# Side work of an output phase, rescheduled: one turn and two differences or splits a step, two more token tiles loaded into operands' places, their norm in place

## The chip, the cores and the metric

The kernel runs on one core of one Trainium2 chip. Its time is device time in microseconds of one execution. The profile was taken of one further execution of the same program. Engines are named as in the profile: PE (TensorE matmul), PEld (its weight loads), DVE (VectorE), ACT (ScalarE), POOL (GpSimd) and SP (SyncE, which here only issues DMAs).

## The reference

One adaLN-conditioned block over 2048 tokens of width 640, all float32: a state-space convolution (S4), then a gated feed-forward layer of width 1728.

```python
h = _layernorm(x) * (1 + ca) + sa
x = x + ga * _A_ref(h, ...)            # long convolution by FFT, plus u * Dskip
h = _layernorm(x) * (1 + cb) + sb
# _B_ref
gate = jnp.einsum("bsd,df->bsf", h, w1)
up = jnp.einsum("bsd,df->bsf", h, w3)
out = jnp.einsum("bsf,fd->bsd", _silu(gate) * up, w2)
x = x + gb * out
```

The change touches the seam between the two layers: z, the convolution's last transform, is brought back, added to x, normalized and turned for the feed-forward matmuls.

## The kernel before

The convolution runs first and leaves its spectrum `zs` in DRAM. The feed-forward layer then works in two **pairs** of token chunks. A chunk is 512 tokens, four **token tiles** of 128. The width 640 is five k-tiles of 128, the width 1728 fourteen f-tiles, the last of them half full. For precision each float32 operand is split into two float32r parts, a high one (a cast on ACT) and a low one (a subtraction on DVE), and each product takes three matmuls of 128 x 512.

In a pair the gate and up products of most f-tiles are made by a seven-product scheme (`seven`) that needs, beside the chunks' operands A and B, their differences T1, T2, T4 (`x_sums`, then `x_sum_split`). The results h stay in SBUF. Then comes the **output phase** of the pair (`outputs`, L1217): 28 steps, one for each of 14 f-tiles for the first chunk (c = 0) and then for the second (c = 1). The matmuls of a step take h and w2 of one f-tile into five accumulators, 15 matmuls (10 in a step of the last f-tile, which comes as the twelfth of each chunk, steps 11 and 25).

In the output phase of the first pair, PE, DVE, ACT, POOL and SP's stream keep the order in which the code is written (`InOrder`). Each step n writes, in this order:

- `load(n + 4)`: the DMA of w2 for four steps later, issued by ACT (two half DMAs for the last f-tile);
- `operands(n + 1)`: the next step's casts gh (w2) and uh (h) on ACT, and the low parts gl and ul on DVE. Each has two buffers;
- one of the first chunk's leftover adds (`late.pop`), steps 15 to 19;
- `side(n)`: the side work below;
- the matmuls of step n, which stand on PE behind the side work's.

The side work prepares the second pair (`prepare`, L1305) by tables of step numbers. Token tiles 0 to 3 become chunk A, 4 to 7 chunk B:

- `x_get` (L970, `gets`): SP loads z of a token tile from `zs`, and for tiles 4 to 7 x as well (those of 0 to 3 are loaded earlier). z needs 640 KB. A tile with `homes` takes two operands' places of 64 x 2 x 128 a DMA, ten DMAs of 64 KB. A tile without takes a buffer A of pool `tz`, five DMAs of 128 KB; the four buffers A also hold h of the first ten f-tiles, three to a buffer, so one comes free every three steps.
- `x_mid` (L984, `mids`): 16 small matmuls into two PSUM banks of `psG`, which has three; DVE adds them to x (xm), takes the statistics (st, mv), POOL makes the factors (rs) and stores x to `xs` with a DMA of its own.
- `x_norm` (L999, `norms`): one ACT instruction makes the normalized tile. Its four places are T41, T21, T11 and T31.
- `turn_a`, `turn_b` (`x_turn`, L1014): for one k-tile, four transposes on PE into one `psG` bank, then on ACT the modulation (into `room`) and the high part, on DVE the low part.
- `x_sums` (L1039), `x_sum_split` (L1048): four subtractions on DVE for each of two indices i; then for each difference a cast on ACT and a subtraction on DVE.

Every DMA of SP and ACT takes one of eight semaphores (DMAHW0 to DMAHW7) in turn, and waits until the DMA that had this semaphore before has landed. SP and ACT share the eight. This is called a **lane** below. A DMA that waits holds up all that stands behind it on its engine.

At the last step of chunk c = 0 (step 13) x of the four tiles is loaded back from `xs` into places (`xr`), and one accumulator is copied by ACT to `ob`, which the leftover work turns into place for the output's last 128 columns. The phase runs from 593.07 us, the first matmul of step 0, to 709.68 us, where the second pair's first product begins.

The lines quoted in the profile as L108 are a recorder's call, through which all of this phase goes; groups are told apart by tiles. The name T stands for all of T1 to T4.

Of the kernel before, what the change touches and what calls it, by code (L numbers as in the profile page):

```python
# [9 lines left out]
F32 = mybir.dt.float32  # L10
# [3 lines left out]
OP = mybir.AluOpType  # L14
# [3 lines left out]
P = 128  # L18
# [11 lines left out]
KD = D // P  # L30
# [83 lines left out]
def tile_kernel(ctx: ExitStack, tc: tile.TileContext, a):  # L114
    nc = tc.nc
    V, S, G, PE = nc.vector, nc.scalar, nc.gpsimd, nc.tensor
# [564 lines left out]
    def x_tile():  # L681
        return xp.tile([P, D], F32, name="xm", bufs=6)
# [112 lines left out]
    xp = None  # L795
# [122 lines left out]
    def room(i):  # L918

        return wq.tile([P, 512], F32, name=f"s{i}")  # L920
# [49 lines left out]
    def x_get(j, x, loaded=False, homes=None):  # L970

        if homes:
            zs_ = [pair_tile(n, F32).rearrange("p a b -> p (a b)")[:, :768].rearrange("p (b d) -> p b d", b=2)
                   for n in homes]
        else:
            zs_ = [z_tile()]
        with tc.issue_after(zlast[0].ins):
            if not loaded:
                SQ.dma_start(x, a["x"][j * P:(j + 1) * P, :])
            for i, z in enumerate(zs_):  # L980
                z_load(z, j, range(NDC), SQ, 2 * i)
        return [x, [zs_[b * len(zs_) // 4][:, b % (4 // len(zs_))] for b in range(4)]]
# [13 lines left out]
        got.extend(ln_stats(xp, x))  # L996
        G.dma_start(xs[j], x)

    def x_norm(j, got, tiles):  # L999

        x, _, rstd, bias = got
        xn = xn_tile(j % 4)
        S.activation(xn, x, AF.Identity, scale=rstd, bias=bias)
        tiles.append(xn)

# [27 lines left out]
    def turn_a(q, tiles, k, g):  # L1033
        xraw["A", k], xop["A", k] = x_turn(q, tiles, k, k if k < 4 else 8, g)

    def turn_b(q, tiles, k, g):
        xraw["B", k], xop["B", k] = x_turn(q, tiles, k, 4 + k if k < 4 else 8, g)

    def x_sums(i):  # L1039

        b11, b21, b12, b22 = xraw["A", i], xraw["A", i + 2], xraw["B", i], xraw["B", i + 2]
        V.tensor_tensor(b11, b12, b11, op=OP.subtract)
        V.tensor_tensor(b12, b22, b12, op=OP.subtract)
        V.tensor_tensor(b22, b22, b11, op=OP.subtract)
        V.tensor_tensor(b21, b21, b22, op=OP.subtract)
        xraw["T1", i], xraw["T2", i], xraw["T4", i] = b11, b22, b21

    def x_sum_split(i, names=("T1", "T2", "T4")):  # L1048
        for n in names:
            xop[n, i] = x_split(f"{n}{i}", xraw[n, i])  # L1050
# [27 lines left out]
    def fetch(f, name):  # L1078
        ahead[f, name] = weight(f, name)
# [137 lines left out]
    def outputs(q0, order, hs, side, last):  # L1217


        seq = [(c, f) for c in range(2) for f in order]  # L1220
        n_all, raws, ops, xr, accs, late = len(seq), {}, {}, [], [], []

        def load(n, q=None):
            if n < n_all:
                raws[n] = weight(seq[n][1], "w2", q)

        def gate(n):
            if n < n_all and last and seq[n][0]:
                G.tensor_tensor(raws[n][:, :512], raws[n][:, :512], gbr, op=OP.mult)

        def operands(n):
            if n < n_all:
                c, f = seq[n]
                ops[n] = out_operands(raws.pop(n), hs[c][f], f)

        def tail(q, ob, x):

            pt = bank(1)
            for i in range(4):
                PE.transpose(pt[:, i * P:(i + 1) * P], ob[:, i * P:(i + 1) * P], ident)  # L1240
            for i in range(4):
                V.tensor_tensor(x[i][:, 512:], pt[:, i * P:(i + 1) * P], x[i][:, 512:], op=OP.add)

        in_order[0] = True
        for n in range(4):
            load(n)
        gate(0)
        gate(1)
        operands(0)
        in_order[0] = False  # L1250
        yield
        in_order[0] = True
        for n, (c, f) in enumerate(seq):
            q, pos = q0 + c, n % NFT
            load(n + 4, S)
            operands(n + 1)
            gate(n + 2)
            if late and pos > 0:
                late.pop(0)()
            if pos == (13 if c == 0 else 10):  # L1260
                xr = [x_tile() if c else x_place(n) for n in ("T40", "T20", "T10", "T30")]
                for i in range(4):
                    SQ.dma_start(xr[i], xs[4 * q + i])
            if pos == 0:
                acc = {k: bank(0) for k in (4, 0, 1, 2, 3)}
            side(n)
            terms = ops.pop(n)
            for k in (4, 0, 1, 2, 3):
                for i, (hh, w) in enumerate(terms):
                    lhs, rhs = (hh[:, k * P:(k + 1) * P], w[:, :512]) if k < 4 else (w[:, 512:], hh)  # L1270
                    PE.matmul(acc[k], lhs, rhs, start=(pos == 0 and i == 0),
                              stop=(pos == NFT - 1 and i == len(terms) - 1))
                if pos < NFT - 1:
                    continue

                if k == 4:
                    ob = room(8) if c == 0 or last else xp.tile([P, 512], F32, name="idle", bufs=1)
                    S.activation(ob, acc[4], AF.Copy, scale=modT[:, 2, 4:5])
                    continue
                if last and c:  # L1280
                    V.tensor_tensor(xr[k][:, :512], acc[k], xr[k][:, :512], op=OP.add)
                else:
                    og = hs[c][order[10 + k]]
                    V.tensor_tensor(og, acc[k], gbr, op=OP.mult)
                    late.append(lambda x=xr[k], og=og: V.tensor_tensor(x[:, :512], og, x[:, :512], op=OP.add))
                if c == 0 or not last:
                    continue
                if k == 1:
                    tail(q, ob, xr)
                for i in ((), (0, 1), (2,), (3,))[k]:  # L1290
                    x_out(4 * q + i, xr[i])
            if pos == NFT - 1 and not (c and last):
                def rest_of(q=q, ob=ob, x=xr):
                    tail(q, ob, x)
                    for i in range(4):
                        x_out(4 * q + i, x[i])
                late.append(rest_of)
        side(n_all)
        in_order[0] = False
        yield  # L1300
        for t in late:
            t()
            yield

    def prepare(q0, g, x4):  # L1305


        steps, got, tiles = {}, {}, ([], [])

        def at(n, fn):  # L1310
            steps.setdefault(n, []).append(fn)

        mids = (3, 5, 6, 7, 9, 11, 14, 16)
        norms = (5, 7, 8, 9, 12, 13, 16, 18)
        gets = (0, 0, 1, 2, 3, 5, 7, 10)
        homes = (("xA0", "xA1"), ("xA2", "xA3"), ("xA4", "xB2"), ("xB3", "xB4"))
        for i, n in enumerate(norms):
            at(n, lambda i=i: x_norm(4 * q0 + i, got[i], tiles[i // 4]))
        for i, n in enumerate(gets):
            if i < 4:  # L1320
                at(n, lambda i=i: got.__setitem__(i, x_get(4 * q0 + i, x4[i], True, homes[i])))
            else:
                at(n, lambda i=i: got.__setitem__(i, x_get(4 * q0 + i, x_tile())))
        for k, n in enumerate((10, 10, 11, 11, 12)):
            steps.setdefault(n, []).insert(k % 2, lambda k=k: turn_a(q0, tiles[0], k, g))
        for k, n in zip((4, 0, 2, 3, 1), (20, 20, 21, 21, 22)):
            at(n, lambda k=k: turn_b(q0 + 1, tiles[1], k, g))
        for i, n in enumerate(mids):
            at(n, lambda i=i: x_mid(4 * q0 + i, got[i], g))
        at(24, lambda: fetch(NFT - 1, "wg"))  # L1330
        at(25, lambda: [fetch(0, n) for n in ("wg", "wu")])
        at(22, lambda: x_sums(0))
        at(23, lambda: x_sum_split(0, ("T1", "T2")))
        at(23, lambda: x_sums(1))
        at(24, lambda: x_sum_split(0, ("T4",)))
        at(24, lambda: x_sum_split(1, ("T1",)))
        at(25, lambda: x_sum_split(1, ("T2", "T4")))

        def side(n):
            for fn in steps.get(n, ()):  # L1340
                fn()
        return side
# [147 lines left out]
```

## Time and profile before

| what | us |
|---|---|
| three runs | 977.24, 978.68, 983.92 |
| their median | 978.68 |
| the profiled execution's own time | 978.73 |
| its span in the profile | 976.6 |
| output phase of the first pair in it | 593.07 to 709.68 |

Times inside the profile count from the start of its span. In a row of the timeline the first number is the start, the second the time from the first start to the last end of the instructions merged in the row, and brackets show how long the engine was idle before it and what ended that. A waits row gives the engine that waits, whom it waited for, the total in us, how often, and the longest. PE's own durations overlap (a matmul is shown as 0.39 us while the next starts 0.227 us later), so what a step costs is read from starts.

### The profile page before, as it was taken

Reading aid. Unit: us, or ns where it says so; the run is one execution under the profiler, and the core shown is the slowest. Engines: PE = TensorE matmul, PEld = TensorE weight load, DVE = VectorE, ACT = ScalarE, POOL = GpSimd, SP = SyncE. Lnnn points to the kernel's source line nnn. Section 1 sums busy time; section 2 is a strip of 40 time slices with the busy share of each in tenths; the row PEclk is TensorE's granted clock in tenths of the full one; section 3 lists DMA queues with packets and bytes.
Section 4 is the critical chain, followed back from the end, with each engine's and each line's share of the span. In section 5 each row is a group of like instructions: output and inputs, shape, how many; then the busy total and the mean of one; then the engine's idle time right before and its main releaser. Section 6 shows DMA issues by size and latency. Waiting matters only on the chain.

```text
span 976.6 us, 19962 instructions
## 1 busy us (share of the span) xinstructions
PE 899.5 (92%) x7924; PEld 675.1 (69%) x7924; DVE 704.7 (72%) x1225; ACT 534.6 (55%) x732; POOL 284.1 (29%) x300
## 2 busy tenths in 40 slices
PE   5886788999999997899999999999899999999997
PEld 2442456666666665577888887678688888888786
DVE  5687868999999985678566665675886666664674
ACT  4658578999999933356433332464543333323432
POOL 2832424445544301321222210321142222200341
PEclk9656757999999999999999999999999999999999
DMA  9571273766765788692211115966221121114342
GB/s 271 178 282 68 111 178 102 201 174 204 213 181 176 204 203 243 209 310 97 84 55 54 55 41 149 266 192 209 88 94 55 66 90 54 53 49 132 98 163 108
DMA packets 103888, 140.68 MB, mean 144 GB/s; under 512 B 20884, under 2 KB 62996, under 8 KB 103796
## 3 DMA queue, kind: packets, MB, share of 16 engines
q1 hardware_dynamic: 93012, 113.58, 38.9%
q10 hardware_dynamic: 8480, 18.09, 5.9%
q0 software_dynamic: 2304, 7.74, 2.3%
q8 instruction: 62, 1.02, 0.4%
q14 instruction: 30, 0.25, 0.1%
HBM read 107.92 MB, written 31.46 MB: 143 GB/s over the span
## 4 chain that ended last, share of the span: by engine, by line
PE 64%; ACT 12%; DVE 10%; DMA 7%; issue 3%; SPq 2%; POOL 1%; ACTq 0%; DVEq 0%; POOLq 0%
PE ps L108 46%; PE p L593 6%; ACT cs L142 3%; PE pz L635 3%; PE pt L562 3%; DMA A<-zs 3%; PE pa L455 2%; DMA s<-in_s_dram 2%; PE pk L544 2%; ACT A L142 2%; ACT L142 1%; ACT ph L142 1%; SPq L108 1%; DMA us<-u 1%; DVE E L520 1%
## 5 line engine op out<-in xcount | busy, mean ns | idle before, releaser
L108 DVE TENSOR_TENSOR s<-ps,s 128x512 f32<-128x512 f32 x138 | 94.9, 688 | 83.1 <-PE ps L108 82.9
L108 ACT CAST gh<-rw 128x640 fp32r<-128x640 f32 x87 | 63.4, 728 | 127.9 <-PE ps L108 85.4
L108 DVE TENSOR_TENSOR gl<-rw,gh 128x640 fp32r<-128x640 f32 x87 | 77.9, 895 | 69.5 <-ACT gh L108 69.3
L108 POOL TENSOR_TENSOR S<-rw 128x256 f32<-128x256 f32 x46 | 36.1, 786 | 225.2 <-DVE S0l L108 160.9
L593 PE MATMUL p<-uk,s 128*64 128x256 f32 x640 | 82.2, 401 | 16.0 <-DMA s<-in_s_dram 5.4
L108 PE MATMUL ps<-gh,uh 128*128 128x512 f32 x224 | 88.3, 394 | 0.0
L108 PE MATMUL ps<-gl,uh 128*128 128x512 f32 x224 | 88.2, 394 | 0.0
L108 PE MATMUL ps<-xA,gh 128*128 128x512 f32 x280 | 87.5, 391 | 0.4 <-ACT xA L108 0.4
L491 POOL TENSOR_TENSOR ph<-thi,iota 128x1376 int32<-128x1376 int32 x20 | 50.0, 2503 | 123.9 <-DVE A L531 90.6
L108 PE MATMUL ps<-gh,ul 128*128 128x512 f32 x208 | 81.1, 390 | 0.0
L593 PEld LDWEIGHTS p<-uk,s 128*64 128x64 f32 x640 | 46.6, 142 | 42.7 <-issue 8.1
L142 ACT ACTIVATE A<-pa 128x1024 f32<-128x1024 f32 (+1 forms) x80 | 64.5, 815 | 18.5 <-PE pa L455 18.3
L108 PEld LDWEIGHTS ps<-xA,gh 128*128 128x128 f32 x280 | 52.3, 188 | 12.9 <-issue 1.2
L527 DVE TENSOR_TENSOR A<-A,ph 128x1024 f32<-128x1024 f32 x40 | 54.5, 1363 | 0.9
L562 PE MATMUL pt<-s,K 128*64 128x128 f32 x640 | 51.0, 300 | 3.9 <-ACT uk L145 3.9
L108 PE MATMUL ps<-xA,gl 128*128 128x512 f32 x140 | 54.5, 389 | 0.0
L520 DVE TENSOR_TENSOR E<-A,cs 128x1024 f32<-128x1024 f32 x40 | 53.4, 1335 | 0.6 <-PE pk L544 0.6
L544 PE MATMUL pk<-E 128*32 128x64 f32 x1280 | 46.6, 239 | 4.0 <-DVE E L523 3.0
L108 PEld LDWEIGHTS ps<-gl,uh 128*128 128x128 f32 x224 | 42.6, 190 | 9.2
L635 PE MATMUL pz<-Y,i 64*128 64x128 f32 x640 | 47.3, 288 | 1.7 <-ACT zt L145 1.6
L108 PEld LDWEIGHTS ps<-gh,uh 128*128 128x128 f32 x224 | 42.5, 190 | 9.0
L635 PEld LDWEIGHTS pz<-Y,i 64*128 64x128 f32 x640 | 39.7, 190 | 12.6 <-issue 9.2
(242 smaller groups left out, 2231.9 us busy)
## 6 DMA issues: line engine op xcount, KB each, us to landing
rw<-in_w_dram ACTq DMA_DIRECT2D x44, 320.0 KB
us<-u SPq DMA_DIRECT2D x16, 640.0 KB
s<-in_s_dram SPq DMA_DIRECT2D x40, 256.0 KB
i<-in_i_dram SPq DMA_DIRECT2D x40, 256.0 KB
rw<-in_wg_dram SPq DMA_DIRECT2D x31, 320.0 KB
rw<-in_wu_dram SPq DMA_DIRECT2D x28, 320.0 KB
uk<-us SPq DMA_DIRECT2D x32, 256.0 KB
zs<-zt SPq DMA_DIRECT2D x32, 256.0 KB
```

Of the source, the lines that this page charges most:

```text
L108: ins = fn(*args, **kw)
L142: return tc.keep_in_program_order(S.activation(*args, **kw))
L455: keep(PE.matmul(ps[:, rr, :8 * n], lx[rows, s // SPC, s % SPC // 2, :], table[rows].rearrange("p j b -> p (j b)"), start=True, stop=True, ...
L491: hold(G.tensor_tensor(p[:, :, b0:], bc(thi[:, sl], 2, NPG - b0), bc(iota, 1, 2 * SD), op=OP.mult))
L520: keep(V.tensor_tensor(EC[s][:, :, 1:3, :], AA[s][:, :, 1:3, :], mid(cs[s]), op=OP.mult))
L527: keep(V.tensor_tensor(A[:, :, 1:3, :], A[:, :, 1:3, :], mid(ph[s]), op=OP.mult))
L544: keep(PE.matmul(pk[dq * 32:dq * 32 + 32, g, :], x[:, g * 4 + dq, 1, :], x[:, g * 4 + dq, 0:3:2, :], start=(st == 0), stop=(st == 1), tile ...
L562: keep(PE.matmul(pt[c * 64:c * 64 + 64, g, :], kk[:, g, :], s1[:, c, :], start=True, stop=True, tile_position=(0, c * 64)))
L593: keep(PE.matmul(p2[par * 64:par * 64 + 64, pi, c, :], s2[:, pi * 2 + par, c * 64:c * 64 + 64], uk[:, 0:kn + 1:kn, f, :], start=True, stop ...
L635: ins = keep(PE.matmul(pz[:, par, (g % 2) * 2 + pi, :], i1[r, pi, c, :], Y[r, pi, c, :], start=(c == 0), stop=(c == 1), tile_position=(par ...
```

## The change

All of it is in the first pair's output phase, but for `ob` of the last chunk, and no instruction is computed otherwise than before.

- **gets** go from steps 0, 0, 1, 2, 3, 5, 7, 10 to 0, 0, 1, 2, 3, 4, 4, 6. Tiles 4 and 5 get homes, T40 with T20 and T10 with T30, and so ten DMAs in the place of five.
- **mids** go from 3, 5, 6, 7, 9, 11, 14, 16 to 3, 4, 5, 6, 8, 9, 10, 12; **norms** from 5, 7, 8, 9, 12, 13, 16, 18 to 5, 6, 7, 8, 11, 12, 13, 15.
- The norm of tiles 4 to 7 is written over x itself, so it waits for no place of the first four, but for the store of x to `xs`.
- **Turns** of chunk A go from two at step 10, two at 11, one at 12 to one each at 9 to 13; those of chunk B from 20, 20, 21, 21, 22 to 16 to 20.
- **Differences** go from four at 22 and four at 23 to two each at 20 to 23; **splits** from 23, 23, 24, 24, 25, 25 to two each at 24 to 26.
- `xr` of the first chunk takes T11 in the place of T30, which chunk B's second turn now needs earlier. `ob` always takes its own place, since `room(8)` is needed earlier by a turn of chunk B.

```diff
-    def x_norm(j, got, tiles):
+    def x_norm(j, got, tiles, here=False):
...
-        xn = xn_tile(j % 4)
+        xn = x if here else xn_tile(j % 4)
...
-    def x_sums(i):
+    def x_sums(i, which=range(4)):
...
+        if 0 in which:
+            xraw["s", i] = xraw["A", i], xraw["A", i + 2], xraw["B", i], xraw["B", i + 2]
+        b11, b21, b12, b22 = xraw["s", i]
+        for n in which:
+            to, l, r = ((b11, b12, b11), (b12, b22, b12), (b22, b22, b11), (b21, b21, b22))[n]
+            V.tensor_tensor(to, l, r, op=OP.subtract)
...
-                xr = [x_tile() if c else x_place(n) for n in ("T40", "T20", "T10", "T30")]
+                xr = [x_tile() if c else x_place(n) for n in ("T40", "T20", "T10", "T11")]
...
-                    ob = room(8) if c == 0 or last else xp.tile([P, 512], F32, name="idle", bufs=1)
+                    ob = xp.tile([P, 512], F32, name="idle", bufs=1)
...
-        mids = (3, 5, 6, 7, 9, 11, 14, 16)
-        norms = (5, 7, 8, 9, 12, 13, 16, 18)
-        gets = (0, 0, 1, 2, 3, 5, 7, 10)
-        homes = (("xA0", "xA1"), ("xA2", "xA3"), ("xA4", "xB2"), ("xB3", "xB4"))
+        mids = (3, 4, 5, 6, 8, 9, 10, 12)
+        norms = (5, 6, 7, 8, 11, 12, 13, 15)
+        gets = (0, 0, 1, 2, 3, 4, 4, 6)
+        homes = (("xA0", "xA1"), ("xA2", "xA3"), ("xA4", "xB2"), ("xB3", "xB4"), ("T40", "T20"), ("T10", "T30"),
+                 None, None)
...
-        for k, n in enumerate((10, 10, 11, 11, 12)):
-            steps.setdefault(n, []).insert(k % 2, lambda k=k: turn_a(q0, tiles[0], k, g))
-        for k, n in zip((4, 0, 2, 3, 1), (20, 20, 21, 21, 22)):
-            at(n, lambda k=k: turn_b(q0 + 1, tiles[1], k, g))
...
+        for k in range(KD):
+            at(9 + k, lambda k=k: turn_a(q0, tiles[0], k, g))
+        for n, k in enumerate((4, 0, 2, 3, 1)):
+            at(16 + n, lambda k=k: turn_b(q0 + 1, tiles[1], k, g))
...
-        at(22, lambda: x_sums(0))
-        at(23, lambda: x_sum_split(0, ("T1", "T2")))
-        at(23, lambda: x_sums(1))
-        at(24, lambda: x_sum_split(0, ("T4",)))
-        at(24, lambda: x_sum_split(1, ("T1",)))
-        at(25, lambda: x_sum_split(1, ("T2", "T4")))
+        for i in range(2):
+            for n in range(4):
+                at(20 + 2 * i + n // 2, lambda i=i, n=n: x_sums(i, (n,)))
+        for j, (i, n) in enumerate(((0, "T1"), (0, "T2"), (0, "T4"), (1, "T1"), (1, "T2"), (1, "T4"))):
+            at(24 + j // 2, lambda i=i, n=n: x_sum_split(i, (n,)))
```

Three places show what moved. The first is SP's stream behind z of tile 3. T_6796 and T_6797 are T40 and T20, T_6858 and T_6859 are T10 and T30, A the buffers of `tz`, xm a place for x.

```order
 L108 DMA xm<-in_x_dram 128x640
-L108 DMA A<-zs 64x4x128 x5
-L108 DMA xm<-in_x_dram 128x640
-L108 DMA A<-zs 64x4x128 x5
...
+L108 DMA T_6796<-zs 64x2x128 x5
+L108 DMA T_6797<-zs 64x2x128 x5
+L108 DMA xm<-in_x_dram 128x640
+L108 DMA T_6858<-zs 64x2x128 x5
+L108 DMA T_6859<-zs 64x2x128 x5
+L108 DMA xm<-in_x_dram 128x640
```

Between the x of tile 4 and the x of tile 6 there stood 11 DMAs on SP, and there stand 21 now.

The second place is ACT in steps 5 to 7, with the semaphores that each instruction waits for; rw is the place of w2, gh and uh the next step's high parts, T the normalized tile. Before:

```order
L108 DMA rw<-in_w_dram 128x640 [waits DMAHW5_49,DVE_49]
L108 CAST gh<-rw 128x640 [waits PE_49]
L108 CAST uh<-A 128x512
L108 ACTIVATE T_6876<-xm,rs 128x640 [waits Pool_49]
L108 DMA rw<-in_w_dram 128x640 [waits DMAHW3_49,DVE_49]
...
L108 DMA rw<-in_w_dram 64x640 [waits DMAHW5_49,DVE_49]
L108 DMA rw<-in_w_dram 64x640 [waits DMAHW6_49]
```

And in the changed kernel:

```order
L108 DMA rw<-in_w_dram 128x640 [waits DMAHW2_49,DVE_49]
L108 CAST gh<-rw 128x640 [waits PE_49]
L108 CAST uh<-A 128x512
L108 ACTIVATE T_6927<-xm,rs 128x640 [waits Pool_49]
L108 DMA rw<-in_w_dram 128x640 [waits DMAHW4_49,DVE_49]
...
L108 ACTIVATE T_6977<-xm,rs 128x640 [waits Pool_49]
L108 DMA rw<-in_w_dram 64x640 [waits DMAHW3_49,DVE_49]
L108 DMA rw<-in_w_dram 64x640 [waits DMAHW5_49]
```

The w2 loads took other lanes: counted along SP's stream from x of tile 4 as DMA 0, the lane of step 5's load was held last by DMA 4 (z of tile 4), that of step 6's by DMA 13, those of step 7's two by DMAs 20 and 21 (all three z of tile 5). Step 8's load, further on, has the lane of the first of step 7's two, and step 9's that of x of tile 7.

The third place is DVE at the end of the phase; s are the raw operands of which the differences are made, T their low parts. Before, from the last turn's low part (step 22) on:

```order
L108 TENSOR_TENSOR T_7632<-s_7630,T_7632 128x512
L108 TENSOR_TENSOR s_7123<-s_7549,s_7123 128x512
L108 TENSOR_TENSOR s_7549<-s_7585,s_7549 128x512
L108 TENSOR_TENSOR s_7585<-s_7585,s_7123 128x512
L108 TENSOR_TENSOR s_7176<-s_7176,s_7585 128x512
L108 TENSOR_TENSOR gl<-rw,gh 128x640
L108 TENSOR_TENSOR ul<-h,uh 128x512
L108 TENSOR_TENSOR T_7664<-s_7123,T_7664 128x512
```

And in the changed kernel, from the last turn's low part (step 20) on:

```order
L108 TENSOR_TENSOR T_7589<-s_7587,T_7589 128x512
L108 TENSOR_TENSOR s_7141<-s_7468,s_7141 128x512
L108 TENSOR_TENSOR s_7468<-s_7504,s_7468 128x512
L108 TENSOR_TENSOR gl<-rw,gh 128x640
L108 TENSOR_TENSOR ul<-h,uh 128x512
L108 TENSOR_TENSOR s_7504<-s_7504,s_7141 128x512
L108 TENSOR_TENSOR s_7235<-s_7235,s_7504 128x512
L108 TENSOR_TENSOR gl<-rw,gh 128x640
```

Two subtractions now stand between one step's ul and the next step's gl, where four stood.

More of the change, by code (lines that the diff above doesn't have):

```diff
@@ L1037, in turn_b @@
         xraw["B", k], xop["B", k] = x_turn(q, tiles, k, 4 + k if k < 4 else 8, g)
-    def x_sums(i):
[L1041 to L1045, printed above, removed]
+    def x_sums(i, which=range(4)):
[5 more added lines that the diff above has]
+            V.tensor_tensor(to, l, r, op=OP.subtract)
         xraw["T1", i], xraw["T2", i], xraw["T4", i] = b11, b22, b21
@@ L1317, in prepare @@
         for i, n in enumerate(norms):
-            at(n, lambda i=i: x_norm(4 * q0 + i, got[i], tiles[i // 4]))
+            at(n, lambda i=i: x_norm(4 * q0 + i, got[i], tiles[i // 4], i > 3))
         for i, n in enumerate(gets):
[L1320 to L1323, printed above, removed]
-        for k, n in enumerate((10, 10, 11, 11, 12)):
-            steps.setdefault(n, []).insert(k % 2, lambda k=k: turn_a(q0, tiles[0], k, g))
@@ L1326, in prepare @@
-        for k, n in zip((4, 0, 2, 3, 1), (20, 20, 21, 21, 22)):
-            at(n, lambda k=k: turn_b(q0 + 1, tiles[1], k, g))
+            at(n, lambda i=i: got.__setitem__(i, x_get(4 * q0 + i, x4[i] if i < 4 else x_tile(), i < 4, homes[i])))
         for i, n in enumerate(mids):
             at(n, lambda i=i: x_mid(4 * q0 + i, got[i], g))
+        for k in range(KD):
+            at(9 + k, lambda k=k: turn_a(q0, tiles[0], k, g))
+        for n, k in enumerate((4, 0, 2, 3, 1)):
+            at(16 + n, lambda k=k: turn_b(q0 + 1, tiles[1], k, g))
```

## The prediction

> **What bounds the kernel now.** I read the page first, then the stretches around the output phase of the first pair, then PE's waits there, and last the rows around each wait.
>
> ```profile
> span 976.6 us, 19962 instructions
> PE 64%; ACT 12%; DVE 10%; DMA 7%; issue 3%; SPq 2%; POOL 1%; ACTq 0%; DVEq 0%; POOLq 0%
> ```
>
> PE carries the chain. A change of side work can only win back what PE waits for, or make PE wait. The stretches (busy us, number of instructions, then granted clock, DMA share, GB/s):
>
> ```profile
> core 0: us, PE busy (x) PEld busy (x) DVE busy (x) ACT busy (x) POOL busy (x), PEclk, DMA share, GB/s
> 609.00:632.00 23.00, 22.41 (x141) 15.05 (x140) 14.81 (x30) 10.71 (x16) 9.20 (x20) 1.00 1.05 252
> 632.00:646.00 14.00, 12.28 (x74) 9.31 (x73) 9.22 (x18) 8.70 (x15) 2.72 (x5) 1.00 1.01 300
> 690.00:698.80 8.80, 5.44 (x22) 3.63 (x20) 8.59 (x13) 5.48 (x10) 0.00 (x0) 1.00 0.14 39
> 698.80:702.80 4.00, 3.95 (x11) 3.08 (x12) 3.83 (x6) 0.43 (x2) 0.00 (x0) 0.59 0.47 157
> ```
>
> The reader is to see two different troubles: from 609 to 646 us the DMA engines are full, at the end DVE is (8.59 of 8.80 us), and there the clock falls. PE's waits in the phase, 588 to 702 us:
>
> ```profile
> engine line waited for: us in total, times, longest us
> PE ps L108 <- DVE uh L108: 2.2, 1, 2.2
> PE ps L108 <- ACT s L108: 1.7, 1, 1.7
> PE ps L108 <- DVE gl L108: 1.1, 1, 1.1
> PE ps L108 <- DVE xm L108: 0.6, 1, 0.6
> ```
>
> That is all: four waits, 5.6 us. PE's own rows place them and give the price of a step:
>
> ```profile
> 593.07 0.39 PE L108 MATMUL ps<-uh,gh 128*128 128x512 f32 x1
> 596.47 0.39 PE L108 MATMUL ps<-uh,gh 128*128 128x512 f32 x1
> ...
> 603.36 0.88 PE L108 MATMUL ps<-xA,i 64*32 64x256 f32 x16
> 607.71 0.39 PE L108 MATMUL ps<-uh,gh 128*128 128x512 f32 x1
> ...
> 616.85 0.52 PE L108 MATMUL ps<-xA,i 64*32 64x384 f32 x3 [0.59 <-DVE xm L108]
> ...
> 634.27 1.03 PE L108 MATMUL ps<-ident,T 128*128 128x128 f32 x8
> 638.60 1.03 PE L108 MATMUL ps<-ident,T 128*128 128x128 f32 x8
> 641.90 0.87 PE L108 MATMUL ps<-A,i 64*32 64x384 f32 x14 [1.72 <-ACT s L108]
> ...
> 692.81 0.49 PE L108 MATMUL ps<-uh,gl 128*128 128x512 f32 x1 [1.11 <-DVE gl L108]
> ...
> 698.85 0.50 PE L108 MATMUL ps<-uh,gh 128*128 128x512 f32 x1 [2.20 <-DVE uh L108]
> ...
> 700.22 0.63 PE L108 MATMUL ps<-gh,uh 128*128 128x512 f32 x1
> 700.64 0.63 PE L108 MATMUL ps<-gl,uh 128*128 128x512 f32 x1
> ```
>
> A bare step takes 3.40 us (593.07 to 596.47). One with a mid takes 4.4 us (603.36 to 607.71, and 0.1 before its first matmul). Two turns make a step 4.33 us (634.27 to 638.60), so one costs 0.47 us. The change keeps all of these: eight mids, ten turns, 28 steps. PE's work is the same.
>
> **What the change removes.** The sum is made against the profiled execution's 978.73 us, 0.05 us above the median.
>
> 1. Differences two a step. DVE's rows before the longest wait:
>
> ```profile
> 694.48 2.86 DVE L108 TENSOR_TENSOR s<-s,s 128x512 f32<-128x512 f32 x4
> 697.26 0.82 DVE L108 TENSOR_TENSOR gl<-rw,gh 128x640 fp32r<-128x640 f32 x1
> 698.11 0.69 DVE L108 TENSOR_TENSOR uh<-h,uh 64x512 fp32r<-64x512 f32 x1
> ```
>
> Four differences hold DVE 2.86 us, and gl and the half tile's low part, for which PE waits, stand behind them. With two, DVE has in a step gl and ul (1.4), two differences (1.4) and at step 20 a low part (0.6): 3.4 us against PE's 3.4 to 3.9. Both late waits go: 1.11 + 2.20 = 3.3 us. Two splits a step at 24 to 26 are 1.2 us of DVE and as much of ACT: no cost.
>
> 2. The half clock. From 699.43 to 702.78 us eight matmuls come every 0.43 us (700.22 to 700.64) where 0.227 is the rule, in the stretch whose granted clock is 0.59. That costs 8 x 0.20 = 1.6 us. It follows the 2.20 us wait closely, and the 1.72 us wait alone had no such sequel, so I count it as gone: 1.6 us.
>
> 3. One turn a step. At 641.90 PE waited 1.72 us for a PSUM bank that ACT had not yet emptied after a second turn. That goes: 1.7 us. The 0.59 us at 616.85 goes in its old form (term 5).
>
> Together 7.2 us. The in-place norm saves no instruction; its wait for x's store to `xs` has the three steps between mid and norm, over 12 us, where the slower landing quoted under 4 took 6.50, so it costs nothing.
>
> **What the change adds.** 4. SP's stream. Its rows at the place where the new DMAs stand, and the chain's two rows that tell how long a DMA takes from issue to landing:
>
> ```profile
> 599.14 9.76 SPq L108 DMA_DIRECT2D xB<-zs  x15
> 609.01 0.54 SPq L108 DMA_DIRECT2D xm<-in_x_dram  x1
> 609.64 3.64 SPq L108 DMA_DIRECT2D A<-zs  x5
> ```
>
> ```profile
> 597.84 2.85 DMA xA<-zs
> 612.24 6.50 DMA A<-zs
> ```
>
> SP needs 0.65 us a DMA (9.76 / 15), whether 64 KB or 128 KB. With x of tile 4 issued at 609.01 as before, DMA number k behind it issues at 609.0 + 0.65 k: number 4 at 611.6, 13 at 617.5, 20 at 622.0, 21 at 622.65. ACT's w2 loads of steps 5, 6 and 7 wait for their landings, l later. l for these 64 KB is what the trace does not show: 2.85 us with the engines half busy, 6.50 us (for 128 KB) with them full. SP would move 20 x 64 KB and 2 x 320 KB in 14.3 us, 137 GB/s; w2 and the stores to `xs` add 74 GB/s each at 320 KB in 4.4 us. That is 286 GB/s where the full stretch moved 252. The backlog after 14.3 us would be 0.49 MB, 1.9 us, on average 1 us. I take l = 2.85 + 1.25 = 4.1 us, nearer the low end.
>
> What PE then waits is read from the like of it:
>
> ```profile
> 613.90 0.33 ACTq L108 DMA_DIRECT2D rw<-in_w_dram  x1
> 614.27 0.73 ACT L108 CAST gh<-rw 128x640 fp32r<-128x640 f32 x1 [3.22 <-DMA xm<-in_x_dram]
> ...
> 615.78 0.68 DVE L108 TENSOR_TENSOR ul<-A,uh 128x512 fp32r<-128x512 f32 x1
> 616.38 0.88 DVE L108 TENSOR_TENSOR xm<-ps,xm 128x256 f32<-128x256 f32 x2
> ```
>
> ACT's load went late, at 613.90, and with it gh, gl, ul and, behind ul, the adds that empty a mid's banks; PE went on at 616.85. So a load at L lets the next step's matmuls start at L + 2.2 (third matmul needs ul, at L + 2.6), and the next mid pass its second bank at L + 2.95.
>
> 5. Step by step, with l = 4.1. Mids now stand in steps 3, 4, 5 and 6 in a row. Step 4's mid, at 607.7, waits for the bank of step 3's: the load there went at 605.18, so until 608.1: 0.45 us. Step 5 begins at 612.5, its mid free. Step 5's load goes at 611.6 + 4.1 = 615.7, and step 6's mid, at 616.9, waits until 618.6: 1.65. Step 6's load, at 617.5 + 4.1 = 621.6, lets step 7 go at 623.8 where it would at 622.95: 0.8. Step 7's second half load, at 622.65 + 4.1 = 626.75, with 0.25 for the second issue, lets step 8's matmuls go at 629.2 where they would at 628.15: 1.05. Step 8's load waits for the first half load of step 7 (626.1 + 4.1 = 630.2), and step 9's second bank comes at 633.15 where PE is at 632.65: 0.5. Step 9's load waits for x of tile 7, some 633.5, and step 10's mid comes only at 638. Sum 4.45 us. The same lines give 2.7 us at l = 2.85, and at l = 6.5, where eight lanes allow one DMA every 0.81 us, 12.45 us.
>
> z itself comes in time: tile 5 lands by 627 us for a mid at 632.6.
>
> 6. Step 13 to 14. Norm, turn and the copy to `ob` now share step 13 on ACT:
>
> ```profile
> 635.62 0.78 ACT L108 ACTIVATE s<-ps,modT 128x512 f32<-128x512 f32 x1
> ...
> 636.95 0.77 ACT L108 ACTIVATE s<-ps,modT 128x512 f32<-128x512 f32 x1
> ...
> 649.20 0.73 ACT L108 CAST gh<-rw 128x640 fp32r<-128x640 f32 x1 [0.70 <-PE ps L108]
> ...
> 651.18 0.67 ACT L108 ACTIVATE s<-ps,modT 128x512 f32<-128x512 f32 x1
> ```
>
> Before, gh to the end of `ob` took 2.65 us; a turn put ahead adds 1.33 (635.62 to 636.95) and the load 0.4: 4.4 us against a step of 3.87, and step 14's first matmul needs the bank that `ob` empties, now without a mid ahead of it. I take 0.6 us; the bounds are nothing and this.
>
> Sum: 978.73 - 7.2 + 4.45 + 0.6 = **976.6 us**, 2.1 us less. With l = 2.85 and term 6 it is 974.8; with l = 6.5, 984.6; with no wait of terms 4 to 6 at all, 971.5.
>
> **A rule beside the clock term.** The Trainium skill (TensorE: Matmul & The Clock Gate, Why this matters for your kernels) asks only for no idle gaps above about 3 us between matmuls. By that rule waits of 1.11 and 2.20 us would not have halved the clock, the 1.6 us would stay, and the sum would be 978.2 us. The trace has the half clock 0.6 us behind a 2.20 us wait, and I follow the trace.
>
> **The rivals.**
>
> - *ACT held by full lanes: slower.* If DMAs of 64 KB take over 4.7 us to land in steps 5 to 8, the new waits exceed 7.2 us (between 5.05 us at 4.1 and 13.05 at 6.5, by line), and the time passes 978.73; at 6.5 it is 984.6. For it: DMA share 1.05 in that stretch, and more DMAs of half the size ask for more than was moved. Against: smaller DMAs put less in flight, and a waiting PE asks for less. Its range alone is 979 to 988; the upper end is two half-clock stretches more.
> - The Trainium skill (DMA: Bandwidth & Descriptors, Rules for kernel authors) speaks for this rival: many small transfers should be coalesced, those under 64 KB being mostly overhead. No run here shows yet what the halving does.
> - *No new wait at all.* The loads of steps 5 to 8 find their lanes free. Against it: before, a load was already late at 613.90. 971.5 us.
> - *The late waits stay*, since DVE at 3.4 us in step 20 is as full as PE: then 4.9 us are not won, 981.5 us. Against it: steps 21 to 23 have 0.6 us to spare each.
> - *The half clock stays* at some other place: 978.2 us.
>
> **How the numbers follow.** The forecast (l from 2.85 to 4.7 us, 974.8 to 978.7) has 0.58, the slower rival 0.27, no new wait 0.07, late waits 0.05, half clock 0.03. The predicted time is the forecast's, 976.6. The range of 972.5 to 984.5 leaves out most of the 971.5 and the upper half of the slower rival, 0.19 in all. About 1%, 9.8 us, is what a measurement of this kernel can tell from no change: faster than 968.9 is out of reach of every case, 0.01; above 988.5 needs the slower rival with several half-clock stretches, 0.04; within, 0.95.
>
> **What would show it.** Right: no wait on DVE's gl or uh above 0.3 us in the last eight steps and the clock at 1.00 there (terms 1, 2); none on ACT's s at the turns (3); ACT's w2 issues in steps 5 to 8 behind z's landings by the clock times above, with PE waits of 1 to 2 us there (4, 5); about 0.6 us at step 14 (6). Wrong: a PE wait for z's DMA itself, for an in-place norm, or w2 issues later than 4.7 us behind DMAs 4, 13 and 21.

## The result and the profile after

The changed kernel takes 975.26 us (median of 20 runs, 969.75 to 978.10), the kernel before 977.77 us (20 runs, 972.95 to 983.92): a ratio of 0.9967, 95% interval 0.9952 to 0.9983, so 1.7 to 4.7 us less; the two medians by themselves are 2.5 us apart. The profiled execution took 976.36 us with a span of 974.6 us, 2.0 us less than the span before; 2.1 us were forecast.

PE's waits in the phase, 588 to 702 us, of the changed kernel:

```profile
PE ps L108 <- ACT uh L108: 2.5, 2, 1.4
PE ps L108 <- ACT idle L108: 0.2, 1, 0.2
```

None of the four waits of before is left. In their place PE waits twice for uh, ACT's cast of h. The stretches (busy us, granted clock, DMA share, GB/s; the third is a part of the second):

```profile
609.00:632.00 23.00, 20.31 (x131) 12.80 (x130) 13.88 (x29) 7.46 (x11) 7.38 (x20) 1.00 0.85 244
632.00:646.00 14.00, 14.00 (x82) 10.08 (x83) 10.57 (x22) 7.37 (x11) 5.09 (x10) 0.88 1.01 299
631.90:635.30 3.40, 3.31 (x8) 2.64 (x9) 1.31 (x3) 2.04 (x3) 0.00 (x0) 0.51 1.10 325
690.00:698.80 8.80, 8.80 (x40) 7.29 (x39) 7.38 (x12) 3.56 (x7) 0.00 (x0) 1.00 0.50 167
698.80:702.80 4.00, 4.00 (x19) 3.32 (x18) 3.47 (x6) 4.00 (x8) 0.00 (x0) 1.00 0.26 95
```

The last two were the trouble at the end: PE is now busy for all of their 12.8 us, where it was for 9.4, and at the full clock. The trouble is at 609 to 632 us instead, 20.31 us busy for 22.41, with a new half clock behind it. PE's rows show the start of the phase, both waits, the matmuls every 0.43 us behind the second, and the end:

```profile
595.09 0.39 PE L108 MATMUL ps<-uh,gh 128*128 128x512 f32 x1
...
624.68 0.50 PE L108 MATMUL ps<-uh,gh 128*128 128x512 f32 x1 [1.12 <-ACT uh L108]
625.02 0.50 PE L108 MATMUL ps<-uh,gl 128*128 128x512 f32 x1
625.63 0.50 PE L108 MATMUL ps<-ul,gh 128*128 128x512 f32 x1
...
631.04 0.50 PE L108 MATMUL ps<-uh,gh 128*128 128x512 f32 x1 [1.37 <-ACT uh L108]
...
633.00 0.63 PE L108 MATMUL ps<-gl,uh 128*128 128x512 f32 x1
633.43 0.63 PE L108 MATMUL ps<-gh,ul 128*128 128x512 f32 x1
...
707.65 0.62 PE L108 MATMUL ps<-xA,gh 128*128 128x512 f32 x2
```

The phase takes 707.65 - 595.09 = 112.56 us, where it took 709.68 - 593.07 = 116.61. So the change won 4.05 us in this execution, and 2.0 us of it were lost ahead of the phase: it starts 2.02 us later, though not an instruction differs there. At 422 us the two executions are 0.24 us apart, though each has some 7 to 10 us at half clock shortly before, at different places (382.06 to 385.47 and 402.54 to 405.95 us before, 396.42 to 406.66 in the changed kernel). Between 426 and 441 us, where z of the first pair is brought back, the changed kernel's execution falls behind by 1.8 us; PE's rows, before and after:

```profile
422.24 0.88 PE L108 MATMUL ps<-A,i 64*32 64x256 f32 x16
441.06 1.20 PE L108 MATMUL ps<-ident,T 128*128 128x128 f32 x9 [1.06 <-ACT T L108]
```

```profile
422.48 0.88 PE L108 MATMUL ps<-A,i 64*32 64x256 f32 x16
428.22 0.87 PE L108 MATMUL ps<-A,i 64*32 64x384 f32 x14 [0.25 <-DMA A<-zs]
...
443.08 1.20 PE L108 MATMUL ps<-ident,T 128*128 128x128 f32 x9 [1.29 <-ACT T L108]
```

In fourteen profiled executions, those of the experiments with them, the phase starts between 591.47 and 598.66 us, all with the same work ahead of it. That is more than the whole effect, so each run below is judged by the phase's length and its steps first, and by its median second. Behind the phase nothing is won or lost: to the end of the span it is 266.1 to 267.0 us in the five profiles of the two kernels.

ACT's rows tell why uh is late. ACTq is the issue of a DMA, and a bracket holds ACT's idle time, with the w2 load's wait in it:

```profile
615.81 0.35 ACTq L108 DMA_DIRECT2D rw<-in_w_dram  x1
616.21 0.73 ACT L108 CAST gh<-rw 128x640 fp32r<-128x640 f32 x1 [3.63 <-DMA T<-zs]
...
622.95 0.34 ACTq L108 DMA_DIRECT2D rw<-in_w_dram  x1
623.38 0.72 ACT L108 CAST gh<-rw 128x640 fp32r<-128x640 f32 x1 [5.11 <-DMA T<-zs]
...
628.29 1.35 ACTq L108 DMA_DIRECT2D rw<-in_w_dram  x2
629.74 0.72 ACT L108 CAST gh<-rw 128x640 fp32r<-128x640 f32 x1 [4.29 <-PE ps L108]
```

ACT stands for 5.11 us until a DMA of z into T has landed, though gh needs only w2, which was loaded four steps earlier: the load written ahead of gh waits for that DMA's lane. (The third bracket names PE. The load at 628.29 goes 0.07 us behind the landing of DMA 20, so there too it was the lane.)

The steps in us, from the start of a step's first matmul, its side work's included, to that of the next step's, show where time goes; a wait ahead of a step's first matmul counts with the step before it. A bare step is 3.40 (2.27 for steps 11 and 25), a mid adds 0.95 to 1.05, a turn 0.48. The columns are the profiles of before (with its second one, before_again), of the changed kernel (with after_again and after_timed) and of w2_pool and w2_pool_mids, all told below.

| step | before | | changed | | | w2_pool | w2_pool_mids |
|---|---|---|---|---|---|---|---|
| 4 | 3.49 | 3.49 | 4.77 | 4.67 | 4.81 | 4.45 | 4.45 |
| 6 | 5.89 | 5.03 | 5.63 | 6.57 | 8.72 | 4.36 | 4.36 |
| 7 | 4.88 | 4.67 | 4.11 | 4.12 | 4.00 | 3.49 | 3.49 |
| 8 | 3.49 | 3.49 | 7.93 | 6.35 | 5.44 | 4.45 | 4.45 |
| 9 | 4.36 | 4.36 | 4.84 | 5.97 | 5.61 | 4.84 | 4.75 |
| 10 | 4.33 | 4.29 | 4.75 | 4.75 | 4.75 | 8.33 | 3.97 |
| 11 | 6.52 | 5.39 | 2.85 | 2.85 | 2.85 | 2.85 | 3.62 |
| 24 | 7.53 | 6.66 | 3.40 | 3.40 | 3.40 | 3.40 | 3.40 |
| 25 | 3.93 | 3.95 | 2.27 | 2.27 | 2.27 | 2.27 | 2.27 |
| phase | 116.61 | 113.45 | 112.56 | 112.95 | 113.88 | 110.45 | 107.19 |

### The profile page after: what moved, and what is told of

The parts are those of the page before. It is cut to its first block, busy times and chain, and to the rows that moved or that the text cites. A ratio compares the mean times of both kernels' runs of the same rounds, so it can differ in the third digit from the quotient of the medians.

```text
span 974.6 us, 19972 instructions
## 1 busy us (share of the span) xinstructions
PE 902.0 (93%) x7924; PEld 676.4 (69%) x7924; DVE 704.6 (72%) x1225; ACT 534.3 (55%) x732; POOL 281.9 (29%) x300
## 4 chain that ended last, share of the span: by engine, by line
PE 70%; ACT 10%; DMA 6%; DVE 6%; SPq 4%; issue 3%; POOL 1%; DVEq 0%; ACTq 0%; POOLq 0%
PE ps L108 49%; PE p L593 6%; SPq L108 3%; PE pz L635 3%; PE pt L562 3%; ACT cs L142 3%; PE pa L455 2%; PE pk L544 2%; DMA s<-in_s_dram 2%; ACT A L142 2%; DMA A<-zs 2%; ACT ph L142 1%; PE pm L306 1%; ACT L142 1%; ACT uk L145 1%
## 5 line engine op out<-in xcount | busy, mean ns | idle before, releaser
L562 PEld LDWEIGHTS pt<-s,K 128*64 128x64 f32 x640 | 40.4, 151 | 12.6 <-ACT uk L145 7.0
```

The source lines that it names most:

```text
L562: keep(PE.matmul(pt[c * 64:c * 64 + 64, g, :], kk[:, g, :], s1[:, c, :], start=True, stop=True, tile_position=(0, c * 64)))
```

## The experiments

Theory A, the prediction's: the gain is DVE's at the end of the phase, where the late waits go; the loss is ACT's, which stands behind w2 loads that wait for lanes held by z's many DMAs.

**Both kernels once more** (after_again, before_again): no edit.

> The changed kernel itself, profiled once more, to see what of its phase repeats. Theory A: steps 4 and 6 to 8 lose 4 to 6 us again, in whichever of them the landings fall; steps 21 to 27 are bare; the half clock at step 8 may be absent. Phase 111 to 114 us. Rival (the waits of steps 6 to 8 are an accident of one execution): phase below 109 us.

> The kernel before, profiled once more. Theory A: step 24 again loses about 4 us to DVE; the half clock behind it, and the wait of step 6, may be larger or absent. Phase 114 to 119 us. Rival (the late waits are an accident of one execution): step 24 below 5 us.

Measured: 112.95 us for the changed kernel, 113.45 for the one before. What repeats is the late wait of before (step 24: 6.66 us, with the half clock in step 25) and the loss of the changed kernel in steps 4 to 9; neither is an accident. What does not repeat is its spread over the steps, the half clock at step 8, and 1.1 of the 2.3 us that step 11 lost before. With before_again the two kernels are 0.5 us apart, with the first profiles 4.05: one pair of profiles does not tell the size of this change.

**The late part undone** (late_undone): in the changed kernel, the late tables as they were.

```diff
-        for i in range(2):
-            for n in range(4):
-                at(20 + 2 * i + n // 2, lambda i=i, n=n: x_sums(i, (n,)))
...
+        at(22, lambda: x_sums(0))
+        at(23, lambda: x_sum_split(0, ("T1", "T2")))
+        at(23, lambda: x_sums(1))
...
```

> The changed kernel with its differences and splits written as before (four at 22, four at 23). Theory A (the gain sits there, since DVE with four differences a step overruns PE): the phase, 112.56 us in the changed kernel, grows by 2 to 6 us, with PE waits on DVE at steps 23 to 25 again, and the median goes from 975.3 to 977 to 981. It may be less than the 5.8 us that steps 24 and 25 cost before, since here no turn's low part stands in step 22. Rival (the late waits came from the late turns of chunk B, not from the four differences a step): no wait above 0.5 us in steps 22 to 26, phase within 0.5 us of 112.56.

Measured: 978.65 us, ratio to the kernel before 0.9992 (0.9963 to 1.0020); phase 114.33 us, step 24 at 5.20, step 25 at 2.42, steps 21 to 23 bare. PE's two longest waits in the phase:

```profile
PE ps L108 <- DVE uh L108: 1.6, 1, 1.6
PE ps L108 <- ACT uh L108: 1.1, 1, 1.1
```

The late wait comes back, on DVE and in its place, but with 1.80 + 0.15 = 1.95 us, and no half clock behind it. Steps 24 and 25 lost 5.8 us before with a half clock, 4.3 in before_pool (below) without. So the differences alone don't explain the late waits: in this kernel the turns of chunk B, whose low parts are DVE's, are already done at step 20. The phase grew by 1.8 us over the first changed profile, a little under the 2 that were expected; the rival, no wait above 0.5 us, is out.

**The late part alone** (b_late): in the kernel before, two differences a step at 21 to 24 and two splits at 24 to 26, turns of chunk B left at 20 to 22.

```diff
-        at(22, lambda: x_sums(0))
...
+                at(21 + 2 * i + n // 2, lambda i=i, n=n: x_sums(i, (n,)))
...
+            at(24 + j // 2, lambda i=i, n=n: x_sum_split(i, (n,)))
...
```

> The kernel before with two differences a step (21 to 24) and two splits a step (24 to 26), and nothing else of the change. Theory A: steps 24 and 25 lose their 4.13 + 1.66 us, the phase goes from 116.6 to about 110.9 us and the median from 977.8 to about 972, below the changed kernel. Rival (the late work cannot be spread so while chunk B is turned at 20 to 22): the waits come back at 21 to 24, phase above 114 us.

Measured: 977.30 us, ratio 0.9970 (0.9942 to 0.9999); phase 113.87 us. Steps 24 and 25 are bare, but steps 23 and 26 lose 1.03 and 0.98 us to DVE. So of the 4.3 us spreading the differences alone leaves 2.0, moving the turns alone leaves 1.95 (late_undone), and both together nothing: each is worth a good half. The 110.9 us of the expectation were not reached, nor the rival's 114. Step 6 shows the lanes at work without any of the change:

```profile
620.65 0.66 PE L108 MATMUL ps<-xA,i 64*32 64x384 f32 x3 [1.92 <-DVE xm L108]
```

It cost 8.76 us here, with a half clock behind it, for 5.89 and 5.03 in the two profiles of before. Such executions may be why the median shows less than the late steps win; only this one was seen.

**One turn a step as well** (b_late_turns): the run before, with turns of chunk A one each at 10 to 14, the norm of tiles 4 to 7 in place, and `ob` in its own place.

```diff
-        for k, n in enumerate((10, 10, 11, 11, 12)):
-            steps.setdefault(n, []).insert(k % 2, lambda k=k: turn_a(q0, tiles[0], k, g))
+        for k in range(KD):
+            at(10 + k, lambda k=k: turn_a(q0, tiles[0], k, g))
...
```

> The kernel before with all of the change but the earlier gets, mids and norms and the homes of tiles 4 and 5: differences and splits as in the run before, turns of chunk A one each at 10 to 14, norm in place, ob in its own place. Theory A (one turn a step takes away the wait on ACT's s, which by the starts of steps is 2.26 us and not 1.72): phase about 108.6 us, median about 970. By the wait rows alone 109.2. Rival (the wait is the mid's behind a turn, two PSUM banks for three users, and comes back wherever a mid and a turn share a step, now steps 11 and 14): phase about as with the late part alone, 110.5 to 111.5.

Measured: 978.72 us, ratio 0.9982 (0.9950 to 1.0015); phase 111.51 us. Steps 10 to 14 together take 21.67 us, in b_late 21.41: spreading the turns alone won nothing. Step 11 falls from 5.39 to 3.75 us, close to the 3.62 of w2_pool_mids for the same work, so its wait does go. But step 14, where a turn, a mid and the bank that `ob` empties come together, rises from 4.36 to 6.26, of which 4.84 are work. The rival was right on this point. The phase is shorter than b_late's by step 6, 5.15 us for 8.76, which the edit does not touch, and steps 22 and 23 give back 0.9 us of that.

**w2 by POOL** (w2_pool): in the changed kernel, the first pair's w2 loads of the phase are issued by POOL, whose DMAs take semaphores of their own.

```diff
-            load(n + 4, S)
+            load(n + 4, S if last else G)
```

> The changed kernel with the first pair's w2 loads of the output phase issued by POOL, whose DMAs have lanes of their own, so that ACT waits for no lane. Theory A (the held ACT costs steps 4 and 6 to 8 some 5.6 us with the half clock behind them): no wait on ACT uh in steps 6 to 9, no half clock there, phase 107 to 108 us, median 970 to 971. Rival (PE waits there for the data of z or for DVE, and lanes are only at the same time): the waits stay, phase 111.5 or more. Second rival: POOL pays for each issue and its factors rs come late, so mids and norms slip, phase 110 or more with PE waits on other tiles.

Measured: 973.03 us, ratio 0.9933 (0.9904 to 0.9961); phase 110.45 us. Steps 4, 6, 7 and 8 hold what their mids need and nothing more. That settles the cause of the waits: the same casts, mids and DMAs of z, with no lane shared, cost PE nothing there. The 107 to 108 us of the expectation were not reached. The second rival's number, 110 or more, was, but not by its cause, late factors from POOL: of PE's waits two are left, one new:

```profile
PE ps L108 <- DMA A<-zs: 1.4, 1, 1.4
PE ps L108 <- ACT idle L108: 0.2, 1, 0.2
```

PE now comes to tile 6's mid in step 10 before its z, with a half clock behind that wait, and step 10 takes 8.33 us for 4.75:

```profile
641.40 0.87 PE L108 MATMUL ps<-A,i 64*32 64x384 f32 x14 [1.36 <-DMA A<-zs]
...
643.43 0.63 PE L108 MATMUL ps<-uh,gl 128*128 128x512 f32 x1
643.86 0.63 PE L108 MATMUL ps<-ul,gh 128*128 128x512 f32 x1
```

**And two mids later** (w2_pool_mids, pool_mids_again): z of tile 6 is given time.

```diff
-        mids = (3, 4, 5, 6, 8, 9, 10, 12)
-        norms = (5, 6, 7, 8, 11, 12, 13, 15)
+        mids = (3, 4, 5, 6, 8, 9, 11, 13)
+        norms = (5, 6, 7, 8, 11, 12, 14, 15)
```

> The kernel of the run w2_pool with the mids of tiles 6 and 7 later (11 and 13 in the place of 10 and 12) and the norm of tile 6 at 14. Theory A (with ACT free, PE only comes too early for z of tile 6, which landed 1.4 us after PE asked for it in step 10): step 10, 8.33 us there, falls to about 4.0, no half clock, phase 110.45 - 3.5 = 107 us, median 970 to 971. Rival (the DMA engines are full and give the wait back one mid later: z of tile 7, or x of it stored before its norm in place, holds PE or ACT at 13 to 15): phase 109 or more with a wait in steps 13 to 16.

Measured: 972.45 us, ratio 0.9909 (0.9877 to 0.9941); phase 702.68 - 595.49 = 107.19 us, at the full clock throughout. PE's rows at both ends, and the stretch that lost most in the changed kernel, now busy for all of its 23 us:

```profile
595.49 0.39 PE L108 MATMUL ps<-uh,gh 128*128 128x512 f32 x1
...
702.68 0.62 PE L108 MATMUL ps<-xA,gh 128*128 128x512 f32 x2
```

```profile
609.00:632.00 23.00, 23.00 (x161) 15.42 (x159) 15.72 (x33) 10.02 (x15) 12.88 (x28) 1.00 0.87 243
```

The DMA share there is 0.87, for 0.85 in the changed kernel, and 243 GB/s for 244: in this stretch it was not the bandwidth that PE waited for. Something is left at step 14, which takes 4.31 us for 3.40, with the phase's only wait, 0.60 us, for DVE's emptying of an accumulator; tile 7's mid now stands just ahead of it, at step 13. Run once more, beside the changed kernel on one chip:

> The kernel of the run w2_pool_mids once more, beside the changed kernel on one chip. Theory A (its phase is 5.5 us shorter than the changed kernel's, 107.2 against 112.6 to 113): median 4 to 7 us below the changed kernel's of this call, phase 107 to 108 us again. Rival (the one profile was lucky, and landings as late as 7 us hold PE in other executions): phase above 109 us, median within 3 us of the changed kernel's.

> The changed kernel once more, timed beside the kernel before and the run above. Theory A: 0.2 to 0.5 per cent below the kernel before, phase 111 to 114 us with the waits in steps 4 and 6 to 9, late steps bare. Rival (the first interval, 0.9952 to 0.9983, was the chip's): no difference from the kernel before.

Measured: 970.40 us, ratio 0.9915 (0.9885 to 0.9946), phase 107.26 us; the changed kernel beside it 977.14 us, ratio 0.9985 (0.9964 to 1.0007), phase 113.88 us, with a half clock in step 6. So this version is faster than both: each of its six times here, 967.33 to 973.20 us, lies below each of the changed kernel's twelve, 973.48 to 982.54. The changed kernel's phase swings by 1.3 us over three executions, and this one's by 0.07. By itself the changed kernel's second interval reaches no difference; with the first, 0.9952 to 0.9983, it stays at some 1.6 to 2.5 us faster.

**w2 by POOL in the kernel before** (before_pool): the same one-line edit.

> The kernel before with the first pair's w2 loads of the output phase issued by POOL, nothing else. Theory A (before too, ACT was held by a lane at 613.90, and steps 6 and 7 lost 1.4 + 0.4 us by it): steps 6 and 7 fall to about 4.4 us each, phase 116.6 - 1.9 = 114.7 us, the late steps as they were, median about 976. Rival (step 6 waits for the data of z or for DVE's own work): step 6 stays at 5.5 us or more.

Measured: 977.48 us, ratio 0.9966 (0.9941 to 0.9991); phase 111.88 us. The one line in the kernel before wins about as much as the whole change did (0.9967). Steps 6 and 7 fall to 4.45 and 4.36 as expected, and step 11 to 5.39; with that and without a half clock the phase is 2.8 us shorter than expected. Step 24 keeps its waits (7.57 us), with the wait of 2.19 us ahead of step 25, but this time no half clock follows:

```profile
696.40 0.50 PE L108 MATMUL ps<-uh,gh 128*128 128x512 f32 x1 [2.19 <-DVE uh L108]
696.74 0.40 PE L108 MATMUL ps<-uh,gl 128*128 128x512 f32 x1
696.97 0.39 PE L108 MATMUL ps<-gh,uh 128*128 128x512 f32 x1
```

```profile
696.40:699.80 3.40, 3.40 (x15) 2.82 (x16) 3.40 (x6) 1.20 (x3) 0.00 (x0) 1.00 0.46 116
```

**The load behind the casts** (load_behind, load_behind_mids): a cheaper cure was tried, with ACT issuing w2 behind gh and uh; in the second kernel with the later mids too.

```diff
-            load(n + 4, S)
+            if last:
+                load(n + 4, S)
             operands(n + 1)
+            if not last:
+                load(n + 4, S)
```

> The changed kernel with ACT's w2 load of each step of the first pair written behind the next step's casts gh and uh instead of ahead of them; ACT issues it still, on the shared lanes. Theory A (the price is not the lane but what stands behind the waiting load on ACT: gh and uh, for which PE waits): the loads of steps 5 to 7 still go late, but steps 4 to 9 lose at most 1.5 us together in the place of 6; PE then comes early for z of tile 6 in step 10, 1.5 to 3.5 us as in the run w2_pool. Phase 108.5 to 110.5 us, median 972 to 974. Rival (a held ACT costs the same wherever the load stands, since norms, turns and the next casts come behind it): phase 111.5 or more, waits on ACT in steps 6 to 8 again.

> The same, with the mids of tiles 6 and 7 at 11 and 13 and the norm of tile 6 at 14, as in the run w2_pool_mids. Theory A: step 10 is free too, phase 107 to 108.5 us, median 971 to 972.5, the same as with POOL as issuer within 1 us. Rival as above: phase 110 or more.

Measured: 981.93 us, ratio 1.0019 (0.9989 to 1.0049), phase 113.63; and 979.89 us, 1.0005 (0.9977 to 1.0032), phase 113.27. The theory of these two runs fell: the rival's 111.5 us and more, with waits on ACT in steps 6 and 7, came true. Written later, the load takes a lane that a later DMA of SP had (step 5's that of DMA 11, x of tile 5, which landed at 625.11 us), and ACT is held until 625.18 us:

```profile
625.18 0.36 ACTq L108 DMA_DIRECT2D rw<-in_w_dram  x1
625.59 0.92 ACT L108 ACTIVATE T<-xm,rs 128x640 f32<-128x640 f32 x1 [5.51 <-DMA xm<-in_x_dram]
626.42 0.71 ACT L108 CAST gh<-rw 128x640 fp32r<-128x640 f32 x1
```

The hold is some 5 us as before and now has a norm between it and the next gh. An in-order engine that stands for 5 us of a 4.4 us step is late wherever the standing is written; what helps is that it does not stand.

## Why the prediction was right, step by step

The time was right, 976.6 forecast and 975.26 measured, and the mechanism was right in the main, DVE's late waits against ACT's lanes; but both sides of the sum were too small. In the two first profiles 10.0 us went (steps 6 and 7: 1.96, step 11: 2.26, steps 24 and 25: 5.79), where 7.2 were forecast, and 6.25 came (terms 4 to 6), where 5.05 were. That 2.1 us were forecast and the two spans are 2.0 apart is luck: the phase won 4.05 in that pair, and 2.0 were lost ahead of it.

- **Term 1, right in cause, too small.** Steps 21 to 27 are bare and DVE keeps up. But 3.3 us, the two waits' brackets, is not what they cost: step 24 lost 7.53 - 3.40 = 4.13 us, and 4.17 in before_pool. A bracket counts from the modelled end of the matmul before, and the third matmul then waited once more for ul (0.60 us where 0.227 is the rule). And the whole gain was put down to differences two a step, where the earlier turns of chunk B are worth half of it.
- **Term 2, right in size, wrong to be taken as gone.** The half clock cost 1.66 us in step 25 and left that place. But it came back at 631.9 us, for some 1.5 us, and in after_timed in step 6: the rival of a half clock at some other place, given 0.03, came true in two executions of three. A wait of the same length draws it in one execution and not in another (2.20 us in before and 2.19 in before_again, against 2.19 in before_pool), so it should have stood as a chance on every wait above a microsecond, the new ones too. The Trainium skill (TensorE: Matmul & The Clock Gate, What's actually happening) says that the clock is set by an activity window of about 3.4 us that runs freely, so that the same kernel meets it at different phases. The traces agree: the half clock lasted 3.40 us in the stretch 631.90 to 635.30; in the clock records of before, stretches at half clock begin at 382.06, 402.54 and 699.50 us, 6 and then 87 times 3.413 us apart; and a half clock followed waits of 1.36, 1.37, 1.54, 1.88, 1.92, 2.00, 2.19 and 2.20 us, but not others of 1.34, 1.64, 1.72 and 2.19. The Trainium skill's rule of no gaps above about 3 us (TensorE: Matmul & The Clock Gate, Why this matters for your kernels), which the prediction set beside this term, is no safe limit here.
- **Term 3, right that it goes, wrong in what it was.** The changed kernel's step 11 is free of waits, at 2.85 us. But "That goes: 1.7 us" took the whole wait on ACT's s at step 11 for a price of two turns a step. Step 11 cost 6.52 us in that profile and 5.39 in before_again, b_late and before_pool, with the same turns. So of the 2.26 us that it lost the two turns were half (1.13, with a bracket of 0.59). The other 1.13 us were a lane, that of a DMA of z which was issued at 631.14 us and landed 8.27 us later, at 639.41, as ACT's rows show:

```profile
637.76 0.62 ACT L108 CAST xA<-s 128x512 fp32r<-128x512 f32 x1
639.49 0.34 ACTq L108 DMA_DIRECT2D rw<-in_w_dram  x1
639.92 0.72 ACT L108 CAST gh<-rw 128x640 fp32r<-128x640 f32 x1 [1.54 <-PE ps L108]
```

```profile
640.06 0.62 ACT L108 CAST xA<-s 128x512 fp32r<-128x512 f32 x1
640.12 0.33 ACTq L108 DMA_DIRECT2D rw<-in_w_dram  x1
641.06 0.73 ACT L108 CAST gh<-rw 128x640 fp32r<-128x640 f32 x1 [0.38 <-PE ps L108]
```

  The first is before, the second before_again: the load stands 1.1 us behind xA's end in the one, and none in the other. And one turn a step by itself won nothing (b_late_turns): step 11 is freed, and step 14 loses 1.42 us, until the mids too are moved away from it, as in the change.
- **Term 4, right in this profile, not in each.** DMAs 4, 13, 20 and 21 took 2.66, 3.44, 4.20 and 3.84 us from issue to landing, where 4.1 was taken for all, and SP issued one every 0.65 us. In after_timed DMAs 4 and 13, issued at 612.15 and 619.30 us, landed at 617.39 and 624.60: 5.24 and 5.30 us, past the 4.7 that the prediction gave as a sign of being wrong. ACT's loads of steps 5 and 6 in after_timed:

```profile
617.47 0.35 ACTq L108 DMA_DIRECT2D rw<-in_w_dram  x1
624.68 0.33 ACTq L108 DMA_DIRECT2D rw<-in_w_dram  x1
```

- **Term 5, right in cause, in part in place, too small.** ACT's loads of steps 5 to 8 went at 615.81, 622.95, 628.29 and 632.84 us, each at most 0.1 us behind the landing of the DMA whose lane was named, and w2_pool shows that nothing else made PE wait. Against w2_pool's steps, steps 4 and 6 to 9 lost 5.7, 6.1 and 7.0 us in three executions, where 4.45 were forecast. The rule from a load to the third matmul behind it held (2.6 us forecast, 625.63 - 622.95 = 2.68). What was left out is the half clock, in two of the three; without its 1.5 us the first profile lost 4.2, close to the forecast's sum. Where the 1.6 us above the forecast come from in after_again, all at the full clock, stays open. The places moved: the largest item, 1.65 us at step 6's mid, is nothing in the first profile, where PE came to that mid at 619.05 us and not at 616.9, and waits of 1.15 and 2.00 us in the other two.
- **Term 6, right.** Steps 13 and 14 take 4.23 and 3.6 us, for 3.88 and 3.40 with nothing to wait for: 0.55 us, 0.6 forecast.
- **The rivals.** The slower one, ACT held by full lanes, had the right mechanism, and its condition came and went: 4.7 us of landing was not reached in the first profile, and was in after_timed, where term 5 came to 7.0 us. Beside before_again, whose step 11 took 5.39 us, that execution's phase is even longer, 113.88 us for 113.45. The two kernels' phases average 115.03 us (two executions) and 113.13 (three), 1.9 us apart.

## What to carry to other kernels

Ask of every DMA on a compute engine's queue which semaphore it must get back, and from whom: a load whose data nobody needs yet can stop an in-order engine for 5 us, and moving it some lines does not free it, while another issuer does. Read a stall from the starts of whole steps and in more than one execution of each kernel; a wait row names who came last, here "ACT s" and "PE ps" for what a load had held. When an edit spreads work in time and shifts it too, undo each by itself, since either may be enough for most of the gain.

## What the runs showed of the hardware

Half the TensorE clock for 3.4 us followed eight PE waits of 1.36 to 2.20 us and did not follow four of 1.34 to 2.19, in this phase of thirteen profiles, at a cost of some 1.5 us (step 8 of the changed kernel) and 1.66 us (step 25 before). The stretch from 609 to 632 us moved 243 GB/s with PE fully busy and 244 with PE held, at a DMA share of 0.87 and 0.85: busy DMA engines were not what PE waited for there. POOL took 0.54 us to issue a w2 load (three in 1.61 us), SP 0.65 us for a DMA of z; the row is w2_pool's:

```profile
629.61 1.61 POOL L108 DMA_DIRECT2D rw<-in_w_dram  x3
```
